# Hash attention and a PReLU feed-forward block: q loaded in blocks and transposed on VectorE, three small jobs moved to GpSimd

## The chip, the cores and the metric

The kernel runs on one NeuronCore of one Trainium2 chip. The metric is the device time of one execution in microseconds (us); a kernel is given by the median of its runs. A profile is one further execution with the hardware profiler on. Engines are called PE (TensorE), DVE (VectorE), ACT (ScalarE), POOL (GpSimd) and SP (SyncE, which here only issues DMAs).

## The reference

```python
# q, k, v: (4, 8, 768, 64) float32; proj: (64, 6)
q_bits = (np.einsum('bhsd,dk->bhsk', q, proj) > 0)
k_bits = (np.einsum('bhsd,dk->bhsk', k, proj) > 0)
# six bits make a bucket number for each query and each key
mask   = q_bucket[:, :, :, None] == k_bucket[:, :, None, :]
scores = np.where(mask, scale * (q @ k^T), -1e9)
attn   = softmax(scores);  x = attn @ v          # heads side by side: (3072, 512)
h      = x @ w_in                                # w_in (512, 2048)
g      = np.maximum(h, 0) + alpha * np.minimum(h, 0)
out    = g @ w_out                               # w_out (2048, 512)
```

A query attends only to keys in the same hash bucket. Six bits of q and of k are signs of a projection.

## The kernel before

There are 4 × 8 heads, handled as 16 **pairs** of heads of 64 columns each, so that a pair fills 128 partitions. The attention stage is one loop over the pairs `pi`; after it come 60 products of the feed-forward block (the first of them begins in the last pair), which the change does not touch.

**One pair on PE.** `scores(pi)` (L755) makes 12 cells, for 6 key tiles `kc` and 2 query groups `g` of 384. Each cell adds a matmul of hash bits (`kb`, `qb`, bf16) to one of `kT` and `qT`; differing bits push the score far down, so that the exponential is nearly zero. ACT takes each cell out of PSUM with one exponential into `pts[kc]` (L766). Then PE does `hash_bits(pi + 1)` (L710, 16 matmuls, tile `hs`), `turn(pi + 2, "q")` (L681, six transposes of 128x128 into PSUM, tile `tp_q`, which ACT copies out with a factor 2^-20 into `qT`), `attend(pi)` (L788, tile `av`, the product with v) and `totals(pi)` (L801, tile `sm`, the row sums from `accd`).

**q and k.** `load` brings both into `nat` two to three pairs ahead. q goes with the sequence in the partitions in two DMAs of 192 KB and is transposed by PE. k has `BY_BLOCKS = 'k'`: `load_blocks` brings it in four DMAs of 96 KB whose runs are 32 numbers long, ordered so that one DVE instruction that transposes 32x32 blocks (`turn_blocks`, L697) gives `kT`. At the end of a pair ACT squares `qn` and `kn` for a bound on their size (`magnitude`), which frees their buffers.

**One pair on DVE, in this order.** Of `divide(pi - 1)`: transposes of the sums `st`, reciprocals and small copies; `weight_clamp` and `weight_parts` for weight tile `i`; `add_first` (`accp` = key tiles 0 + 1); the rest of `divide`, a transpose `dn` and the scaled output `x`; `weight_sum` of `i` (two instructions, L637 and L640) and `weight_clamp` of `i + 1`; `add_third` (L781, `accp` += tile 2); `add_last` (`accd` = tiles 3 + 4, then += 5); `weight_parts` and `weight_sum` of `i + 1`; `add_total` (`accd` += `accp`, read by `totals`); up to two sums of w_in from `weight_sums(2)` (L658, each 128x512); `turn_blocks` of k for `pi + 2`. Four w_in groups exist, with four sums each: they fall due two at a time in pairs 3, 4, 6, 7, 9, 10, 12 and 13. In pairs 3 and 6 the group is completed by that pair's first `weight_sum`, in pairs 9 and 12 by its second; the other four pairs take the two sums that are left of a group completed in the pair before.

**Hash bits.** ACT writes signs for half the bits in place and the rest beside it (L731). Six small DMAs then move bits to the partitions where they belong: four into `qb` (L736) and two inside `kb` (L738). The first score cell of the next pair reads `qb` of group 0, the second cell `qb` of group 1; the two `kb` transfers are for key tiles 3 to 5, from the seventh cell on.

**Order.** `do(...)` pins an instruction behind whatever its engine was given last. A DMA start that is not inside `do` is free: the build's scheduler may issue it earlier, when it takes its inputs to be ready. Each engine then works through its queue in order. All transfers of the attention stage except two at the very beginning are issued by SP; POOL issues DMAs only in the feed-forward stage (`load_out` and `sum_out`, eight each).

Of the kernel before, what the change touches and what calls it, by code (L numbers as in the profile page):

```python
# [12 lines left out]
AF = mybir.ActivationFunctionType  # L13
ALU = mybir.AluOpType
# [393 lines left out]
def fast_path(  # L408
# [12 lines left out]
    nc = tc.nc  # L421
    P = 128
    B, H, S, D = q.shape
# [13 lines left out]
    DOWN = 2.0 ** -20  # L437
# [5 lines left out]
    do = tc.keep_in_program_order  # L443
    PE, DVE, ACT, POOL = nc.tensor, nc.vector, nc.scalar, nc.gpsimd
# [35 lines left out]
    nat, tr, bits = {}, {}, {}  # L480
    accp, accd, av, vsum, sums = {}, {}, {}, {}, {}

    def load(pi, name):
        b, hp = pairs[pi]
        src = {"q": q, "k": k, "v": v}[name]
        if name == "v":
            t = pool.tile([P, 2, NC * D], F32, name=f"vn{pi}", tag="vn")
            nc.sync.dma_start(t, src[b, 2 * hp : 2 * hp + 2].rearrange("h (p c) d -> p h (c d)", c=NC))
            nat[name, pi] = t
        elif pi > 1 and name in BY_BLOCKS:  # L490
            load_blocks(pi, name)
# [8 lines left out]
        for s in range(2):  # L500
            queue.dma_start(nat[name, pi][:, cs, s], src[b, 2 * hp + s].rearrange("(p c) d -> p c d", c=NC)[:, cs])

    BY_BLOCKS = 'k'

    def load_blocks(pi, name):
        b, hp = pairs[pi]
        src = {"q": q, "k": k}[name]
        nat[name, pi] = t = pool.tile([P, NC * 4, 32], F32, name=f"{name}n{pi}", tag=f"{name}n", bufs=3)
        for s in range(2):
            for h in range(2):  # L510
                a = D * s + 32 * h
                nc.sync.dma_start(
                    t[a : a + 32].rearrange("i (c u) d -> i c u d", u=4),
                    src[b, 2 * hp + s, :, 32 * h : 32 * h + 32].rearrange("(u i c) d -> i c u d", u=4, c=NC),
                )
# [39 lines left out]
    raw, wx, wr = {}, {}, {}  # L555
# [22 lines left out]
    def load_weight(i):  # L578
        if i < NW:
            i = order[i]  # L580
            raw[i] = pool.tile([P, 512], moe_w_in.dtype, name=f"raw{i}", tag="raw", bufs=3)
            nc.sync.dma_start(raw[i], piece(i))
# [19 lines left out]
    def weight_clamp(i):  # L602
        if i < NW:
            i = order[i]
            x = wx[i]
            do(DVE.tensor_scalar(x, x, HI_MIN, None, op0=ALU.max, op1=ALU.max, accum_out=wmax[:, i : i + 1]))

    def weight_parts(i):
        i = order[i]
        x = wx[i].bitcast(U32)  # L610
        turned = i < HW and i % 4 == 3
        do(DVE.tensor_scalar(
            x, x, 3, 0x40000000 if turned else 0xC0000000, op0=ALU.logical_shift_left, op1=ALU.bitwise_xor,
        ))
# [29 lines left out]
    def weight_group(i):  # L644

        i = order[i]
        if i >= HW:
            n, m = divmod(i - HW, 2)
            if m == 1:
                nc.sync.dma_start(w_out_r[:, :, n].rearrange("m p d -> p m d"), wst[HW + n])  # L650
            return
        n, m = divmod(i, 4)
        if m < 3:
            return
        w = wst[n]

        def one(to, a, op, c):
            do(DVE.tensor_tensor(w[:, to], w[:, a], w[:, c], op=op))  # L658

        def store():  # L660
            c, kk = divmod(n, 2)
            for ii in range(4):
                nc.sync.dma_start(w_in_s[4 * c + ii][:, :, kk], w[:, :, ii])


        for x in ((3, 5, 2), (5, 0, 5), (4, 3, 0), (6, 1, 4)):
            sums_due.append((one, (x[0], x[1], ALU.subtract, x[2])))
        sums_due.append((store, ()))
# [9 lines left out]
    def two_banks(name):  # L678
        return psum.tile([P, 2, 512], F32, name=name, tag="sc", bufs=3)
# [28 lines left out]
    def hash_bits(pi, halves=BOTH, engine=None):  # L708

        if halves.start == 0:
            bits["q", pi] = qbs[pi % 2]
            kb = pool.tile([P, 3 * CW], BF16, name=f"kb{pi}", tag="kb", bufs=1)
            bits["k", pi] = kb[:, :S]
            bits["raw", pi] = kb.rearrange("p (a w) -> p a w", w=CW)
        ps = {"k": two_banks(f"hs{pi}")}
        ps["q"] = psum_av.tile([P, 2, 512], F32, name=f"hsq{pi}", tag="av") if engine is DVE else ps["k"]
        for half in range(halves.start, halves.stop):
            for name in "qk" if engine is DVE else "kq":  # L720
                for s in range(2):
                    r, c = D * s, D * (s ^ half) + 32 * "kq".index(name)

                    for t, c in [("k", c)] + ([("q", c ^ D)] if engine is DVE and name == "q" else []):
                        do(PE.matmul(
                            ps[t][c : c + 32, half if t == "k" or engine is not DVE else 0, :CW], wh[r : r + D],
                            tr[name, pi][r : r + D, half * CW : (half + 1) * CW], start=True, stop=True,
                        ))
        if engine is None:
            raw = bits["raw", pi]  # L730
            do(ACT.activation(raw[:, 0:3:2], ps["k"][:, :, :CW], AF.Sign, bias=hb))  # L731
            for half in range(2):
                for s in range(2):
                    c = D * (s ^ half)
                    cols = slice(half * CW, (half + 1) * CW)
                    nc.sync.dma_start(bits["q", pi][D * s : D * s + 32, cols], raw[c + 32 : c + 64, 2 * half])  # L736
                    if half:
                        nc.sync.dma_start(bits["k", pi][D * s : D * s + D, cols], raw[c : c + D, 2])  # L738
            return
        for half in range(halves.start, halves.stop):  # L740
            cols = slice(half * CW, (half + 1) * CW)
            for s in range(2):
                c = D * (s ^ half ^ (engine is DVE)) + 32
                do(ACT.activation(
                    bits["q", pi][D * s : D * s + 32, cols], ps["q"][c : c + 32, 0 if engine is DVE else half, :CW], AF.Sign, bias=hb[c : c + 32],
                ))

            for to, c, n in [(0, 0, P)] if half == 0 else [(0, D, D), (D, 0, D)]:
                dst, src = bits["k", pi][to : to + n, cols], ps["k"][c : c + n, half, :CW]
                do(DVE.tensor_scalar(  # L750
                    dst, src, hb_k[c : c + n, 0:1], hb_k[c : c + n, 1:2], op0=ALU.is_gt, op1=ALU.subtract,
                ))
# [16 lines left out]
    def p(kc):  # L769
        return pts[kc].rearrange("p g s w -> p (g s) w")[:, :, :CW]  # L770

    def add_first(pi):
        accp[pi] = pool.tile([P, 2 * NCH, CW], F32, name=f"accp{pi}", tag="accp", bufs=1)
        do(DVE.tensor_tensor(accp[pi], p(0), p(1), op=ALU.add))  # L774
# [4 lines left out]
        do(DVE.tensor_tensor(accd[pi], accd[pi], p(5), op=ALU.add))  # L779

    def add_third(pi):  # L781
        do(DVE.tensor_tensor(accp[pi], accp[pi], p(2), op=ALU.add))  # L782

    def add_total(pi):
        do(DVE.tensor_tensor(accd[pi], accd[pi], accp[pi], op=ALU.add))  # L785
# [375 lines left out]
    for pi in range(NPAIR):  # L1161
        i = 2 * pi

        def weight_begin():
            weight_clamp(i)
            weight_parts(i)
            add_first(pi)

        scores(pi, [c for c in CELLS if pi or c not in ahead])
        if pi:  # L1170
            divide(pi - 1, weight_begin)
        else:
            add_first(pi)
        weight_sum(i)
        weight_group(i)
        load_weight(i + 3)
        if pi == 0:
            weight_abs(1, DVE)
        weight_clamp(i + 1)
        add_third(pi)  # L1180
        add_last(pi)
        weight_parts(i + 1)
        weight_sum(i + 1)
        weight_group(i + 1)
        load_weight(i + 4)
        add_total(pi)
        weight_sums(2)
        if pi + 1 < NPAIR:
            hash_bits(pi + 1)
        if pi + 2 < NPAIR:  # L1190
            for name in "qk":
                (turn_blocks if name in BY_BLOCKS else turn)(pi + 2, name)
        attend(pi)
        if pi + 1 == NPAIR:
            now = ff1(0, 0)
            now.step(1)
        totals(pi)
        if pi + 1 == NPAIR:
            now.step(5)
            divide(pi)  # L1200
        else:
            weight_abs(i + 2)
        if pi + 2 < NPAIR:
            load(pi + 2, "v")
        if pi in (9, 11, 15):
            load_w((9, 11, 15).index(pi))
        if pi in (9, 10, 12):
            load_x(0, *{9: (0,), 10: (2, 3), 12: (1,)}[pi])
        if 11 <= pi < 14 or pi == 15:
            sum_x(0, min(pi - 11, 3), DVE)  # L1210
        if pi == 1:
            setup_alpha()
        for name in "qk":
            magnitude(pi, name)
            if pi + 3 < NPAIR:
                load(pi + 3, name)
        if pi + 1 < NPAIR:
            weight_abs(i + 3)
# [97 lines left out]
```

## Time and profile before

| | us |
|---|---|
| median of 3 runs | 892.92 (892.18 to 896.64) |
| the profiled execution | 890.84 |
| its span, first to last instruction | 888.9 |
| DVE busy, 1280 instructions | 758.2 |
| ACT busy, 654 instructions | 369.1 |
| POOL busy, 30 instructions | 14.4 |
| attention stage, until the first product `f_0a` | 333.6 |
| one DVE transpose of q or k (`kT<-kn`), mean | 0.97 |
| one sum of w_in on DVE (`wsi`), mean | 0.69 |

Busy time is a share of the span by engine; it does not say which engine holds the others up, which is read from the waits and from the order in time. The starts of `add_first` (L774), once per pair, mark the period of the attention loop. In the order of the pairs they are 15.78, 34.94, 55.11, 75.06, 96.19, 116.15, 136.10, 157.40, 177.65, 197.32, 217.27, 237.22, 258.64, 279.35, 300.60 and 320.18 us: 19.95 us in an undisturbed pair, up to 21.4 in others.

### The profile page before, as it was taken

The numbers are of one execution on the slowest core, as the hardware profiler recorded it, in microseconds if no ns is written. First come the engines' busy times: TensorE is split into PE (matmuls) and PEld (weight loads), VectorE is DVE, ScalarE is ACT, GpSimd is POOL, SyncE is SP. The second block draws the span as 40 slices with busy tenths as digits, with TensorE's granted clock in tenths as the row PEclk, the third lists the DMA queues.
The fourth block names the chain that finished last, engine by engine and source line by source line (L and its number), as shares of the span: only waits on it lengthen the run. The fifth ranks groups of instructions, "written<-read, shape, count | busy, mean of one in ns | idle before, by whom it ended". The sixth has DMA issues, their size and how long they took to land.

```text
span 888.9 us, 15214 instructions
## 1 busy us (share of the span) xinstructions
PE 874.4 (98%) x5802; PEld 589.5 (66%) x5802; DVE 758.2 (85%) x1280; ACT 369.1 (42%) x654; POOL 14.4 (2%) x30
## 2 busy tenths in 40 slices
PE   9999999999999999999999999999999999999996
PEld 5444544544444445558996558997557997557996
DVE  5899999899989987899898768898668988668895
ACT  7877777777777743221112222112222112222111
POOL 1000000000000001210000000000000000000000
PEclk9999999999999999999999999999999999999999
DMA  8655686687795616677334434434435343520242
GB/s 219 169 133 137 169 229 158 154 218 210 210 266 153 201 48 222 213 281 289 106 122 118 141 118 157 146 107 125 149 115 163 110 146 87 172 98 1 95 155 63
DMA packets 148130, 137.23 MB, mean 154 GB/s; under 512 B 100928, under 2 KB 132176, under 8 KB 144464
## 3 DMA queue, kind: packets, MB, share of 16 engines
q1 hardware_dynamic: 143328, 126.59, 47.0%
q0 software_dynamic: 2304, 8.39, 2.5%
q10 hardware_dynamic: 2416, 1.18, 0.5%
q8 instruction: 48, 0.79, 0.4%
q14 instruction: 34, 0.28, 0.1%
HBM read 104.87 MB, written 28.31 MB: 150 GB/s over the span
## 4 chain that ended last, share of the span: by engine, by line
PE 83%; DVE 8%; DMA 4%; issue 2%; SPq 1%; ACT 1%; DVEq 0%; ACTq 0%
PE sc L763 12%; PE av L796 10%; PE f_0a L896 2%; PE z_4a L896 2%; PE z_3a L896 2%; PE z_7a L896 2%; PE z_5a L896 2%; PE z_6a L896 2%; PE f_4a L896 2%; PE f_3a L896 2%; PE f_1a L896 2%; PE f_2a L896 2%; PE z_2a L896 2%; PE f_5a L896 2%; PE z_1a L896 2%
## 5 line engine op out<-in xcount | busy, mean ns | idle before, releaser
L766 ACT ACTIVATE pt<-sc 128x768 f32<-128x768 f32 x192 | 154.6, 812 | 47.7 <-PE sc L763 46.9
L763 PE MATMUL sc<-qT,kT 64*128 64x384 f32 x768 | 155.7, 483 | 0.0
L796 PE MATMUL av<-pt,vn 128*32 128x385 f32 (+1 forms) x1536 | 127.4, 486 | 0.0
L763 PEld LDWEIGHTS sc<-qT,kT 64*128 64x128 f32 x768 | 70.0, 187 | 41.5 <-issue 41.1
L796 PEld LDWEIGHTS av<-pt,vn 128*32 128x32 f32 x1536 | 48.9, 109 | 70.9 <-issue 70.1
L763 PE MATMUL sc<-qb,kb 64*128 64x384 bf16 x384 | 66.1, 323 | 4.8 <-DMA qb<-kb 4.1
L949 DVE TENSOR_TENSOR g<-g,g 128x384 f32<-128x384 f32 x128 | 68.4, 555 | 2.2
L1013 DVE TENSOR_TENSOR gs<-g,gs 128x768 f32<-128x768 f32 x56 | 53.3, 953 | 1.0
L1005 DVE TENSOR_TENSOR ws<-wl 128x512 f32<-128x512 f32 x56 | 38.5, 687 | 18.3 <-DMA wl<-w_out_s 17.1
L1013 DVE TENSOR_TENSOR gs<-g 128x768 f32<-128x768 f32 x56 | 53.3, 952 | 0.0
L945 DVE SCALAR_TENSOR_TENSOR g<-h,alpha 128x384 f32<-128x384 f32 x32 | 19.7, 616 | 25.1 <-ACT h L938 25.1
L774 DVE TENSOR_TENSOR accp<-pt,pt 128x1536 f32<-128x1536 f32 x16 | 28.1, 1759 | 13.2 <-ACT pt L766 13.2
L763 PEld LDWEIGHTS <-kb 64*128 64x128 bf16 x384 | 21.0, 94 | 27.7 <-issue 4.4
L596 ACT ACTIVATE wr<-raw 128x512 int32<-128x512 uint32 x32 | 22.8, 711 | 26.6 <-issue 25.8
L779 DVE TENSOR_TENSOR accd<-accd,pt 128x1536 f32<-128x1536 f32 x16 | 28.1, 1759 | 1.7
L782 DVE TENSOR_TENSOR accp<-accp,pt 128x1536 f32<-128x1536 f32 x16 | 28.1, 1753 | 0.0
L785 DVE TENSOR_TENSOR accd<-accd,accp 128x1536 f32<-128x1536 f32 x16 | 28.0, 1752 | 0.0
L778 DVE TENSOR_TENSOR accd<-pt,pt 128x1536 f32<-128x1536 f32 x16 | 28.0, 1751 | 0.0
L896 PE MATMUL f_0a<-x,wi 128*128 128x384 f32 x64 | 23.5, 489 | 0.0
L896 PE MATMUL f_1a<-x,wi 128*128 128x384 f32 x64 | 23.3, 486 | 0.0
L896 PE MATMUL f_4a<-x,wi 128*128 128x384 f32 x64 | 23.3, 486 | 0.0
L896 PE MATMUL f_2a<-x,wi 128*128 128x384 f32 x64 | 23.3, 486 | 0.0
(348 smaller groups left out, 1698.1 us busy)
## 6 DMA issues: line engine op xcount, KB each, us to landing
wi<-w_in_s SPq DMA_DIRECT2D x32, 896.0 KB, 4.7
wl<-w_out_s SPq DMA_DIRECT2D x16, 1024.0 KB, 4.8
wl<-w_out_r SPq DMA_DIRECT2D x12, 1024.0 KB, 4.9
raw<-in_moe_w_out_dram SPq DMA_DIRECT2D x16, 512.0 KB, 4.3
raw<-in_moe_w_in_dram SPq DMA_DIRECT2D x16, 512.0 KB, 4.0
w_in_s<-wsi SPq DMA_DIRECT2D x16, 448.0 KB, 5.4
vn<-in_v_dram SPq DMA_DIRECT2D x16, 384.0 KB, 4.5
x_s<-x SPq DMA_DIRECT2D x16, 384.0 KB, 2.6
```

The costliest lines, as they stand in the source:

```text
L763: do(PE.matmul(sc[:, s, :CW], what["k", pi][r, ks], what["q", pi][r, qs], start=first, stop=not first,))
L766: do(ACT.activation(pts[kc][:, g, :, :CW], sc[:, :, :CW], AF.Exp, scale=SCALE / DOWN))
L774: do(DVE.tensor_tensor(accp[pi], p(0), p(1), op=ALU.add))
L778: do(DVE.tensor_tensor(accd[pi], p(3), p(4), op=ALU.add))
L779: do(DVE.tensor_tensor(accd[pi], accd[pi], p(5), op=ALU.add))
L782: do(DVE.tensor_tensor(accp[pi], accp[pi], p(2), op=ALU.add))
L785: do(DVE.tensor_tensor(accd[pi], accd[pi], accp[pi], op=ALU.add))
L796: do(PE.matmul(av[pi][D * s + t : D * s + t + 32, g, :w], nat["v", pi][:, s, kc * D + t : kc * D + t + 32], pts[kc][:, g, s, :w], start=(k ...
L896: do(PE.matmul(self.ps[bank], self.left(left, k), self.right(right, k), start=start and k == 0, stop=k == self.nk - 1, skip_group_check=no ...
L949: do(DVE.tensor_tensor(new_g(b, to)[:, i], g_m[b, x][:, i], g_m[b, y][:, i], op=ALU.subtract))
L1005: do(DVE.tensor_tensor(t, w2[b, n, x], w2[b, n, y], op=op))
L1013: do(DVE.tensor_tensor(t, g2[b, n, x], g2[b, n, y], op=ALU.subtract))
```

## The change

q joins k in `BY_BLOCKS`. For pairs 2 to 15 q is then loaded by four DMAs instead of two, PE's six transposes per pair and ACT's copy out of PSUM go, and one DVE transpose comes in. The factor 2^-20, which ACT's copy applied, is applied by an ACT instruction on `qT` in place, after the hash matmuls have read it. The six hash-bit DMAs of a pair are issued by POOL instead of SP. Two kinds of addition move from DVE to POOL: the sums of w_in and `add_third`.

```diff
-    BY_BLOCKS = 'k'
+    BY_BLOCKS = 'qk'
...
         def one(to, a, op, c):
-            do(DVE.tensor_tensor(w[:, to], w[:, a], w[:, c], op=op))
+            do(POOL.tensor_tensor(w[:, to], w[:, a], w[:, c], op=op))
...
                     cols = slice(half * CW, (half + 1) * CW)
-                    nc.sync.dma_start(bits["q", pi][D * s : D * s + 32, cols], raw[c + 32 : c + 64, 2 * half])
+                    nc.gpsimd.dma_start(bits["q", pi][D * s : D * s + 32, cols], raw[c + 32 : c + 64, 2 * half])
                     if half:
-                        nc.sync.dma_start(bits["k", pi][D * s : D * s + D, cols], raw[c : c + D, 2])
+                        nc.gpsimd.dma_start(bits["k", pi][D * s : D * s + D, cols], raw[c : c + D, 2])
...
     def add_third(pi):
-        do(DVE.tensor_tensor(accp[pi], accp[pi], p(2), op=ALU.add))
+        do(POOL.tensor_tensor(accp[pi], accp[pi], p(2), op=ALU.add))
...
         if pi + 1 < NPAIR:
             hash_bits(pi + 1)
+            if pi:
+                do(ACT.activation(tr["q", pi + 1], tr["q", pi + 1], AF.Copy, scale=DOWN))
         if pi + 2 < NPAIR:
             for name in "qk":
                 (turn_blocks if name in BY_BLOCKS else turn)(pi + 2, name)
```

## The prediction

> **What bounds the kernel now.** I read the page first: busy shares and the chain.
>
> ```profile
> PE 874.4 (98%) x5802; PEld 589.5 (66%) x5802; DVE 758.2 (85%) x1280; ACT 369.1 (42%) x654; POOL 14.4 (2%) x30
> ...
> PE 83%; DVE 8%; DMA 4%; issue 2%; SPq 1%; ACT 1%; DVEq 0%; ACTq 0%
> ```
>
> PE holds the chain for 83%, so work taken from PE can shorten the span. The 8% of DVE and 4% of DMA warn that something else ends close behind. The change touches only the attention loop, so next comes the timeline of one undisturbed pair (pair 2), PE and then DVE.
>
> ```profile
> 61.35 0.88 PE L690 MATMUL tp_q<-ident,qn 128*128 128x128 f32 x6
> 62.16 7.96 PE L796 MATMUL av<-pt,vn 128*32 128x385 f32 x96
> 69.94 0.84 PE L810 MATMUL sm<-accd,ones 128*32 128x192 f32 x16
> ```
>
> ```profile
> 55.11 1.76 DVE L774 TENSOR_TENSOR accp<-pt,pt 128x1536 f32<-128x1536 f32 x1 [0.88 <-ACT pt L766]
> ...
> 58.73 0.68 DVE L637 SCALAR_TENSOR_TENSOR wx<-raw,wx 128x512 uint32<-128x512 uint32 x1
> ...
> 60.66 1.75 DVE L782 TENSOR_TENSOR accp<-accp,pt 128x1536 f32<-128x1536 f32 x1
> ...
> 67.65 1.75 DVE L785 TENSOR_TENSOR accd<-accd,accp 128x1536 f32<-128x1536 f32 x1
> 69.32 0.97 DVE L699 STREAM_TRANSPOSE kT<-kn 128x768 f32<-128x768 f32 x1
> 70.83 0.65 DVE L826 STREAM_TRANSPOSE st<-sm 128x192 f32<-128x192 f32 x2 [0.55 <-PE sm L810]
> ```
>
> From tp_q's start to av's is 0.81 us: what PE pays per pair for transposing q. DVE ends add_total at 67.65 + 1.75 = 69.40, PE starts the sums that read it at 69.94: DVE is only 0.54 early, less than 0.81. In the whole loop of 19.95 us DVE idles 0.88 + 0.55 = 1.4. Pair 14 has no q to turn, so it shows what PE meets without tp_q:
>
> ```profile
> 306.85 7.96 PE L796 MATMUL av<-pt,vn 128*32 128x385 f32 x96
> 315.03 0.86 PE L810 MATMUL sm<-accd,ones 128*32 128x192 f32 x16 [0.21 <-DVE accd L785]
> ```
>
> It waits 0.21 for accd. DVE's chain, not ACT or a DMA, is next, and the answer depends on whether moving add_third really shortens it. Last, waits and DMA issues:
>
> ```profile
> PE sc L763 <- DMA qb<-kb: 4.1, 4, 1.2
> ```
>
> ```profile
> w_out_r<-wso SPq DMA_DIRECT2D x8, 512.0 KB, 4.7
> wo<-w_out_r POOLq DMA_DIRECT2D x8, 512.0 KB, 6.7
> w_out_s<-wo POOLq DMA_DIRECT2D x8, 512.0 KB, 5.6
> qb<-kb SPq DMA_DIRECT2D x60, 24.0 KB, 3.1
> ```
>
> Hash bits are late four times (4.1 us in all), because SP stands at a weight load or store that waits for DVE. POOL's transfers take 0.9 to 2.4 us longer to land than SP's 4.3 to 4.7 for the same size; POOL's own timeline has four issued in 3.12, so 0.78 each.
>
> **What the Trainium skill says.** (1) "SBUF — State Buffer", section "Who interferes with whom": a DVE instruction with two SBUF inputs contends with a GpSimd instruction that reads SBUF, and the one that comes second is blocked until the first is done; a DVE instruction with one SBUF input outside the two-port modes is not. The trace before has no POOL arithmetic in the loop and can't confirm it. (2) "GPSIMD Engine Reference", section 3.1: an fp32 tensor_tensor of 2048 takes 4497 ns on GpSimd against 2293 on DVE. The DVE half fits (1.75 us for 1536 here); the other isn't shown. (3) "DMA: Bandwidth & Descriptors", "SWDGE vs HWDGE vs iDMA": DMAs from GpSimd have their descriptors made by its cores in software; the slower landing above agrees.
>
> **The change, part by part** (L774 starts F are the clock of a pair, S is the start of its scores, F = S + 4.3.)
>
> *q's transposes off PE:* 14 pairs x 0.81 = 11.3 us less PE. ACT's copy (0.80) becomes a copy in place, like the SBUF-to-SBUF pass L706 (0.85): 14 x 0.05, on an engine that idles 1.8 us in the same stretch: nothing. It ends some 7 us before the next scores; without that cover 0.85 per pair.
>
> *q's DVE transpose:* +0.97, after add_total and before the sums are read (st). It fills the 0.55 idle there; the remaining 0.4 comes out of the 0.88 idle ahead of add_first. So nothing, as long as add_total isn't later.
>
> *q's loads:* four issues of about 0.65 instead of two, minus six hash issues (0.58 each): SP gains 2 us per pair. The data are wanted a pair later (about 20 us, landing 3.4 to 4): nothing. The DMA engines were busy 54 to 97% of each pair; 128-byte runs instead of 256 add packets, not bytes. Below 1 us of DMA time per pair, I take nothing.
>
> *Hash bits on POOL:* the signs are ready at S + 11.7. The fifth transfer is the last for qb: four issues x 0.78 later, plus landing. Low bound 3.1 as from SP; high 3.1 + 2.4 = 5.5; I take 4.0 (3.1 + 0.9, the stores' difference): S + 18.8, wanted in the second cell at S + 19.15 + 0.8 = S + 19.95. They fit by 1.1; the 4.1 us of SP's lateness go. POOL's queue ahead of them holds add_third and, in eight pairs, two sums.
>
> *add_third on POOL:* 1536/2048 x 4.5 = 3.4 us (estimate from the skill's GPSIMD page; low bound 1.75 as on DVE). It starts when add_first is done, F + 1.9, and ends F + 5.3. DVE meanwhile does dn and x (one SBUF input each) and comes to L637 at F + 3.62 (58.73 - 55.11), which reads raw and wx, two SBUF inputs: held for 1.7. What the move removes is 1.67 (60.66 to 62.33). Net +0.03: nothing gained on DVE. If nothing is held, -1.67.
>
> *Descriptors:* POOL's six issues lie at F + 7.5 to F + 12.2, and the tensor_scalar L612 (0.42 us for 512, so in a two-port mode) comes at F + 10.7. Held 0 to 0.78, I take 0.3.
>
> *Sums of w_in on POOL:* 512 wide: 1.1 us each. In pairs 4, 7, 10 and 13 they are ready and follow add_third at once, just where DVE goes through L637, L640 (two inputs) and a clamp (one); in pairs 3 and 6 they follow L640 and meet add_last. Taking turns, DVE loses 2 x 1.1 less the 0.6 of the clamp, 1.6. In pairs 9 and 12 they meet add_total: one of them ahead of it, 1.1. DVE's saving of 1.41 comes after add_total, where it only becomes idle time. Low bound nothing.
>
> **The sum.** add_total ends F + 14.29 (69.40 - 55.11) now, F + 14.29 + 0.03 + 0.3 = F + 14.6 after. From there two transposes (1.94) and the row from st to L612 (3.3) to the next F: 19.85, against 19.95. Six early-sum pairs 21.45, pairs 9 and 12 20.95, pair 1 (alpha) 20.05, pair 0 19.0. From the first F to the last: 19.0 + 20.05 + 5 x 19.85 + 6 x 21.45 + 2 x 20.95 = 308.9. Now: 320.18 - 15.78 = 304.4. So +4.5, and 0.3 for pair 15: +4.8. The profiled execution took 890.84 (span 888.9 and 1.9 around it) and would take 895.6; the median of the runs is 2.1 above it, so 897.7.
>
> **Forecast and rivals.**
> - *DVE is held by POOL (forecast, 0.45):* 898, 890 to 908. For it: the 0.21 wait of pair 14 and DVE's 1.4 us of idle per loop. Within it 0.27 slower, 0.17 within, 0.01 faster.
> - *POOL and DVE run side by side (0.30, the other side):* one mechanism, no blocking at L637. add_total ends at F + 12.6, before PE needs it (F + 14.0); PE bounds again: -11.3 - 4.1 gives 877.5, 873 to 884. For it: no trace here shows blocking. The point of decision is the hold: below about 0.7 us per pair DVE keeps ahead of PE. 0.28 faster, 0.02 within.
> - *Hash bits become the bound (0.25):* issues 1.2 apart or queued behind sums, landing 5.5: S + 11.7 + 4.8 + 5.5 = S + 22.0, 2.05 late, 15 times: 31. Less 15.4 gives 908.5, 903 to 930. Against: 0.78 per issue of a transfer twenty times larger. For it: POOL's queue is in order and a DVE that wins every turn starves the sums and with them the bits behind. 0.24 slower, 0.01 within.
>
> Faster 0.29, within 0.20, slower 0.51. 0.5% is 4.5 us, about what a measurement of this kernel can tell from no change. The range 876 to 915 leaves out the fast end of the second case and half of the third, under 0.2; the forecast's own is 890 to 908.
>
> **What would show it.** Right: no tp_q, period near 19.9 in plain pairs and over 21 with sums, L637 with idle time ahead of it or stretched by 1 to 2 us while POOL works, PE waiting for accd at L810. Second case: L637 at F + 3.6 and periods of 19.2. Third: scores waiting on `qb<-kb` in most pairs. What would make it wrong: a POOL add nearer 2 us, or 5.

## The result and the profile after

The changed kernel takes 891.27 us (median of 20 runs, 890.25 to 895.57), the kernel before 892.22 (20 runs beside them): a ratio of 0.9991, 95% interval 0.9978 to 1.0003. That is no change that can be measured. The profiled execution took 891.28; its span is 889.4 us, 0.5 more than before.

The page of the changed kernel: the chain by engine, then three groups with count, busy us, mean ns, and the idle time before them.

```profile
PE 71%; DVE 12%; ACT 6%; issue 4%; DMA 3%; POOL 3%; SPq 0%; DVEq 0%; ACTq 0%; POOLq 0%
...
L782 POOL TENSOR_TENSOR accp<-accp,pt 128x1536 f32<-128x1536 f32 x16 | 51.1, 3194 | 164.1 <-DVE accp L774 164.1
...
L637 DVE SCALAR_TENSOR_TENSOR wx<-raw,wx 128x512 uint32<-128x512 uint32 x32 | 42.3, 1322 | 0.5
...
L658 POOL TENSOR_TENSOR wsi<-wsi 128x512 f32<-128x512 f32 x16 | 29.3, 1834 | 8.5 <-DVE wsi L640 8.0
```

PE's share of the chain fell from 83% to 71%; DVE, ACT and POOL took most of it over. L637 did not change in the source, but its mean went from 688 to 1322 ns. That is the trace of an instruction that is held, which means that it waits while it is counted as running: every other L637 (the one of tile `i`) runs beside `add_third`. Pair 2 in time, DVE and then POOL:

```profile
54.41 1.76 DVE L774 TENSOR_TENSOR accp<-pt,pt 128x1536 f32<-128x1536 f32 x1 [0.45 <-ACT pt L766]
...
58.03 2.04 DVE L637 SCALAR_TENSOR_TENSOR wx<-raw,wx 128x512 uint32<-128x512 uint32 x1
...
66.65 1.75 DVE L785 TENSOR_TENSOR accd<-accd,accp 128x1536 f32<-128x1536 f32 x1
```

```profile
56.35 3.17 POOL L782 TENSOR_TENSOR accp<-accp,pt 128x1536 f32<-128x1536 f32 x1 [10.42 <-DVE accp L774]
62.07 1.50 POOL L736 DMA_DIRECT2D qb<-kb  x3 [2.55 <-ACT kb L731]
```

POOL's add runs from 56.35 to 59.52. L637 begins at 58.03 and ends at 60.07, 0.55 after POOL: nearly all of its own 0.68 comes when the add is over. It is held 1.36 us. `add_total` starts 12.24 after L774, against 12.54 before: of the 1.67 that left DVE, 1.37 came back as waiting.

In pair 3 the two sums of w_in meet `add_last` (DVE, then POOL):

```profile
80.61 2.46 DVE L778 TENSOR_TENSOR accd<-pt,pt 128x1536 f32<-128x1536 f32 x1
83.17 2.65 DVE L779 TENSOR_TENSOR accd<-accd,pt 128x1536 f32<-128x1536 f32 x1
```

```profile
80.16 4.04 POOL L658 TENSOR_TENSOR wsi<-wsi 128x512 f32<-128x512 f32 x2 [1.36 <-DVE wsi L640]
```

Both additions of 1.75 are stretched, by 0.71 and 0.89, and POOL's two sums take 4.04 where 2.62 is enough (the gated kernel below). The two engines take turns here, and `add_total` comes 1.6 later than in pair 2. Pair 9 goes another way (POOL, then PE):

```profile
205.02 0.52 POOL L738 DMA_DIRECT2D kb<-kb  x1
208.17 2.72 POOL L658 TENSOR_TENSOR wsi<-wsi 128x512 f32<-128x512 f32 x1 [2.63 <-DVE wsi L640]
210.85 0.52 POOL L736 DMA_DIRECT2D qb<-kb  x1
```

```profile
211.51 0.32 PE L763 MATMUL sc<-qb,kb 64*128 64x384 bf16 x1
214.50 0.32 PE L763 MATMUL sc<-qb,kb 64*128 64x384 bf16 x1 [2.67 <-DMA qb<-kb]
```

Here the build put a sum between the fourth and the fifth hash-bit transfer. The sum waits for L640, then for `add_total` (208.00 to 209.75), and the last `qb` transfer stands behind it: the second score cell is 2.67 late.

Pair 12 has the same order on POOL, and its second score cell is 1.70 late. But its length comes from somewhere else: there DVE has a sum of x behind the transposes (L868, in pairs 11 to 13), which takes 0.95 alone and is held by the second sum of w_in:

```profile
274.30 2.05 DVE L868 TENSOR_TENSOR x<-x,x 128x768 f32<-128x768 f32 x1
```

DVE has no idle time in this pair before it comes to the next `add_first`, where it idles 0.36, as in a plain pair. So DVE's work, with this hold in it, is as long as the pair (21.28). The late bits can have cost 0.24 at most: the third score cell needs DVE to be done with `st` (276.91, behind L868), and starts at 277.15.

### The profile page after: what moved, and what is told of

It reads as the page before. It is cut to its first block, busy times and chain, and to the rows that moved or that the text cites. A ratio compares the mean times of both kernels' runs of the same rounds, so it can differ in the third digit from the quotient of the medians.

```text
span 889.4 us, 15185 instructions
## 1 busy us (share of the span) xinstructions
PE 864.7 (97%) x5718; PEld 577.0 (65%) x5718; DVE 766.4 (86%) x1262; ACT 370.1 (42%) x654; POOL 140.7 (16%) x152
## 4 chain that ended last, share of the span: by engine, by line
PE 71%; DVE 12%; ACT 6%; issue 4%; DMA 3%; POOL 3%; SPq 0%; DVEq 0%; ACTq 0%; POOLq 0%
PE sc L763 7%; ACT pt L766 5%; PE av L796 4%; PE f_0a L896 2%; PE z_4a L896 2%; PE z_7a L896 2%; PE z_3a L896 2%; PE z_6a L896 2%; PE z_5a L896 2%; PE f_4a L896 2%; PE f_3a L896 2%; PE f_2a L896 2%; PE f_1a L896 2%; PE z_2a L896 2%; PE f_5a L896 2%
## 5 line engine op out<-in xcount | busy, mean ns | idle before, releaser
L782 POOL TENSOR_TENSOR accp<-accp,pt 128x1536 f32<-128x1536 f32 x16 | 51.1, 3194 | 164.1 <-DVE accp L774 164.1
L637 DVE SCALAR_TENSOR_TENSOR wx<-raw,wx 128x512 uint32<-128x512 uint32 x32 | 42.3, 1322 | 0.5
L774 DVE TENSOR_TENSOR accp<-pt,pt 128x1536 f32<-128x1536 f32 x16 | 28.1, 1758 | 8.5 <-ACT pt L766 8.2
L736 POOL DMA_DIRECT2D qb<-kb x60 | 30.2, 506 | 23.0 <-ACT kb L731 20.5
L779 DVE TENSOR_TENSOR accd<-accd,pt 128x1536 f32<-128x1536 f32 x16 | 29.9, 1870 | 2.0 <-ACT wr L596 0.5
L778 DVE TENSOR_TENSOR accd<-pt,pt 128x1536 f32<-128x1536 f32 x16 | 31.4, 1963 | 0.0
L658 POOL TENSOR_TENSOR wsi<-wsi 128x512 f32<-128x512 f32 x16 | 29.3, 1834 | 8.5 <-DVE wsi L640 8.0
```

The source lines that it names most:

```text
L637: do(DVE.scalar_tensor_tensor(x.bitcast(U32), hi, 0x80000000, x.bitcast(U32), op0=ALU.bitwise_and, op1=ALU.bitwise_xor,))
L736: nc.gpsimd.dma_start(bits["q", pi][D * s : D * s + 32, cols], raw[c + 32 : c + 64, 2 * half])
L778: do(DVE.tensor_tensor(accd[pi], p(3), p(4), op=ALU.add))
L782: do(POOL.tensor_tensor(accp[pi], accp[pi], p(2), op=ALU.add))
```

## The experiments

Periods are the distances between the starts of `add_first` in each profile, so each comes from one execution; "loop" is the sum of the 15. A plain pair is pair 2; pair 4 is one with sums. The kernels ran in three groups (e1 to e4, e5 to e8, e9 and e10), each beside runs of the kernel before; ratios are against those.

| kernel | us | ratio (95%) | loop | plain pair | pair 4 |
|---|---|---|---|---|---|
| before | 892.22; beside the three groups 893.94, 893.66, 893.28 | | 304.4 | 19.95 | 19.96 |
| changed | 891.27 | 0.9991 (0.9978 to 1.0003) | 304.9 | 19.28 | 20.72 |
| e1_sums_dve | 886.91 | 0.9930 (0.9906 to 0.9953) | 300.7 | 19.28 | 20.39 |
| e2_q_and_bits | 889.90 | 0.9957 (0.9940 to 0.9973) | 303.9 | 19.59 | 20.69 |
| e3_q_alone | 906.88 | 1.0150 (1.0120 to 1.0179) | 317.8 | 19.65 | 20.69 |
| e4_bits_alone | 887.31 | 0.9933 (0.9909 to 0.9957) | 299.8 | 19.95 | 19.95 |
| e5_sums_gated | 879.29 | 0.9846 (0.9825 to 0.9868) | 293.3 | 19.28 | 19.24 |
| e6_sums_behind_bits | 900.14 | 1.0082 (1.0062 to 1.0102) | 311.1 | 19.29 | 21.64 |
| e7_write_only (sums incomplete) | 874.20, one run | | 288.2 | 19.14 | 19.14 |
| e8_one_input (sums incomplete) | 884.21, one run | | 297.8 | 19.14 | 20.18 |
| e9_gated_clamp | 877.15 | 0.9824 (0.9811 to 0.9837) | 290.3 | 19.14 | 19.15 |
| e10_sum_x_pool | 874.93 | 0.9795 (0.9781 to 0.9808) | 288.9 | 19.14 | 19.15 |

**Taking the change apart.** The diffs of e1 to e3 are against the changed kernel, that of e4 against the kernel before.

```diff
 # e1_sums_dve
-            do(POOL.tensor_tensor(w[:, to], w[:, a], w[:, c], op=op))
+            do(DVE.tensor_tensor(w[:, to], w[:, a], w[:, c], op=op))
 # e2_q_and_bits: that, and
-        do(POOL.tensor_tensor(accp[pi], accp[pi], p(2), op=ALU.add))
+        do(DVE.tensor_tensor(accp[pi], accp[pi], p(2), op=ALU.add))
 # e3_q_alone: both, and the hash bits' two DMA starts
-                    nc.gpsimd.dma_start(...)
+                    nc.sync.dma_start(...)
 # e4_bits_alone: the kernel before, with both DMA starts
-                    nc.sync.dma_start(...)
+                    nc.gpsimd.dma_start(...)
```

> The changed kernel with the sums of w_in back on DVE. Port theory (GpSimd's two-input adds hold DVE's two-input instructions): plain pairs stay at 19.3 us; the eight pairs with sums carry 1.33 of sums on DVE and no hold but add_third's, 20.2 instead of 20.7 to 22.3; pairs 9 and 12 lose their late hash bits. 299 instead of 305 for the loop: 885. Rival, GpSimd's queue (the hash bits behind add_third and the sums cost the time): all pairs near 19.3, 878. Rival, DVE's length alone decides (nothing is held, the sums cost nothing on GpSimd): slower than the changed kernel, 896.

> The changed kernel with both additions back on DVE, so q in blocks and the hash bits on GpSimd remain. Port theory: add_third costs DVE 1.67 instead of a hold of 1.37, so plain pairs take 19.6 and pairs with sums 20.6: 302 for the loop, 889 to 890. L637 is back at 0.69. Rival, GpSimd's queue: without arithmetic in it the bits are on time everywhere, all pairs 19.3, 878. Rival, DVE's length: 1.7 to 3 us per pair more on DVE than in the changed kernel, 900 or more.

> Only q in blocks, everything else as before. Port theory and DVE's length: PE loses 0.81 per pair, but add_total on DVE ends 14.3 after add_first and DVE has one transpose more; plain pairs 19.6, pairs with sums 20.6, and the hash bits from SP are late as before (about 4 in all): 893 to 894, no gain. If PE alone bounded the loop: 881.

> The kernel before with only the hash bits moved to GpSimd. If SP's place in line made them late, the waits of the scores for qb and kb (4.1 us) go and the five long pairs (21.1 to 21.4) fall to 20: 887. If GpSimd's issue or landing is slower than SP's, they stay or grow: 893 or more.

The first and second came out within 2 us of the number of the port theory (GpSimd's additions hold DVE's two-input instructions), and the fourth within 1 us of what it should take if SP's place in line made the bits late. Both rivals fell as the main cause: with no arithmetic in POOL's queue (e2) the pairs with sums are not at 19.3, and with more work on DVE (e1, e2) the kernel is not slower than the changed one. Read as steps of the loop: bits to POOL, 304.4 to 299.8 (-4.6); q in blocks on top, 303.9 (+4.1); `add_third` to POOL, 300.7 (-3.2); the sums to POOL, 304.9 (+4.2). The four cancel. Each step holds for this order alone, and with the other parts as they stand in it: with the bits still on SP, q in blocks costs 13.4 of loop instead of 4.1 (e3). The medians of the runs give -6.6, +2.6 and -3.0 for the first three steps: the same signs, and within 2 us of the loops.

The step with q surprises most. PE lost its 0.81 per pair, and the plain pairs of e2 gained 0.36; but in a pair with sums DVE had little idle (0.27 in e4 at the end of pair 4), and the transpose of 0.97 made pair 4 0.74 longer. In e2 DVE has no idle time at all there. The transpose stands ahead of `st`, and PE shows it as a wait of the third score cell, because `sm`, which `st` reads, and the score cells take turns in the same three PSUM buffers:

```profile
PE sc L763 <- DVE st L826: 9.7, 9, 1.8
```

In e4 this wait is 1.2 in two. It is 0.94 in each of pairs 3, 4, 6, 7, 9 and 10 of e2, and 1.81 in pairs 12 and 13, where a sum of x comes on top. A transpose placed behind `st` was not tried. With the sums taken off DVE and gated (e5, below) these pairs take 19.24 to 19.29: what costs is the transpose together with sums on DVE.

e3 missed its number by 13 us. Its waits on PE name the hash bits, 16.6 us in nine waits; the worst is in pair 11 (SP, then PE):

```profile
248.67 0.59 SPq L663 DMA_DIRECT2D w_in_s<-wsi  x1
254.67 0.38 SPq L650 DMA_DIRECT2D w_out_r<-wso  x1
255.47 0.33 SPq L582 DMA_DIRECT2D raw<-in_moe_w_out_dram  x1
255.85 2.73 SPq L663 DMA_DIRECT2D w_in_s<-wsi  x3
258.68 3.71 SPq L736 DMA_DIRECT2D qb<-kb  x3
```

```profile
264.49 0.58 PE L763 MATMUL sc<-qb,kb 64*128 64x384 bf16 x2 [7.17 <-DMA qb<-kb]
```

The signs were ready at 249.4 (ACT's L731), but SP stood at the store of `wso`, which waits for DVE until 254.64; it issued that store and four more transfers, and the first of the bits only at 258.68. After the wait the granted clock was only 0.50 (264 to 268 us; 1.00 from 270), and pair 11 took 29.48, 9.25 more than in e2. Why the build ordered SP's queue so unluckily in this pair was not followed up; that the bits' place in SP's queue is the danger is what e4 shows from the other side: on POOL, no wait of the scores for bits is left, and of the long pairs of before (21.1 to 21.4) pairs 3, 6 and 11 are at 19.95 and pair 13 at 20.70.

**Where the sums stand.** Two kernels leave them on POOL and move them in its queue. `gate` is a small tile that nothing reads (its declaration is left out here).

```diff
 # e6_sums_behind_bits; e5_sums_gated has the gate too
-        weight_sums(2)
         if pi + 1 < NPAIR:
             hash_bits(pi + 1)
             if pi:
                 do(ACT.activation(tr["q", pi + 1], tr["q", pi + 1], AF.Copy, scale=DOWN))
+        if sums_due and sums_due[0][0].__name__ == "one":     # e5 alone
+            do(POOL.tensor_copy(gate, accd[pi][:, 0, :1]))    # e5 alone
+        weight_sums(2)
```

> The changed kernel with the sums of w_in still on GpSimd, but queued behind the pair's hash bits and behind a one-column copy of accd, which waits for add_total. They then run while DVE does transposes and small one-input instructions. Port theory: no hold but add_third's, all pairs near 19.3, loop 290 instead of 305: 876 to 878. GpSimd's queue as the cause: the same, since the bits are ahead of the sums. DVE's length: no change against the changed kernel, 891.

> As the gated kernel without the gate: sums on GpSimd behind the pair's hash bits, with nothing to make them wait for add_total. They run beside the second half of add_last, weight_sum and add_total. Port theory: DVE is held 1.2 to 1.5 there, pairs with sums 20.6, but pairs 9 and 12 are rid of late bits: 887 to 888. GpSimd's queue as the cause: bits are never behind sums, 878, the same as with the gate.

They differ by one small copy on POOL, and by 21 us. The queue rival wanted them equal; it is out, as is the length of DVE's work, which is the same in both. The gated kernel in pair 3 (POOL, then DVE; its line numbers are two higher):

```profile
87.69 0.18 POOL L1194 COPY gate<-accd 128x1 f32<-128x1 f32 x1 [3.08 <-DVE accd L787]
87.83 2.62 POOL L660 TENSOR_TENSOR wsi<-wsi 128x512 f32<-128x512 f32 x2
```

```profile
87.54 0.97 DVE L701 STREAM_TRANSPOSE qT<-qn 128x768 f32<-128x768 f32 x1
88.44 0.93 DVE L701 STREAM_TRANSPOSE kT<-kn 128x768 f32<-128x768 f32 x1
89.30 0.60 DVE L828 STREAM_TRANSPOSE st<-sm 128x192 f32<-128x192 f32 x2
89.93 0.54 DVE L829 TENSOR_SCALAR rc<-st 128x12 f32<-128x12 f32 x1
```

Two sums take 2.62 instead of 4.04, DVE's transposes run beside them at their own length, and the only thing held is a small one, L829 (0.54 instead of 0.17). Pairs 2 to 10 take 19.24 to 19.29, as expected. Pairs 11 to 13 do not, because of the sum of x on DVE: 19.89, and in pairs 12 and 13, where it meets the gated sums and takes up to 2.02 instead of 0.95, 21.04 and 20.95. Pair 3 without the gate, in e6 (DVE, then POOL):

```profile
84.01 1.93 DVE L612 TENSOR_SCALAR wx<-wx 128x512 uint32<-128x512 uint32 x1
85.97 1.65 DVE L637 SCALAR_TENSOR_TENSOR wx<-raw,wx 128x512 uint32<-128x512 uint32 x1
```

```profile
84.35 2.72 POOL L658 TENSOR_TENSOR wsi<-wsi 128x512 f32<-128x512 f32 x2
```

L612 (0.42 alone) is held by 1.5 and L637 by 0.96, which ends 0.55 behind the second sum.

The port theory's own expectation, 887 to 888, missed by 12, for two reasons. First, it counted two-input instructions alone, and L612 has one. The Trainium skill's page "SBUF — State Buffer", section "Who interferes with whom", says that a DVE instruction in a two-port mode contends with GpSimd too, and names `tensor_scalar` among those that can be; the 1.93 of L612 agrees. `add_total` came 2.4 later than in a plain pair, and PE waited 15.1 us for it in seven pairs.

Second, in pairs 7, 10 and 13 the granted clock fell to 0.50 after that wait (from 176 to 178 us, in pair 7), and four score matmuls took 1.49 instead of 0.81. These pairs took 23.4; pairs 3, 4 and 6, with waits of 2.3 to 2.4 and a clock of 1.00 after them, took 21.6 to 21.8. So some 5 of the 21 us (an estimate, three times 23.4 - 21.7) go with the lower clock. Why it fell in three pairs alone was not followed up.

**What on POOL holds DVE.** Two kernels replace `add_third` by work on POOL that only writes, or that reads one input; the sums of w_in are on DVE. The row sums then leave out key tiles, so these kernels are for the trace alone; each has one run.

```diff
-        do(POOL.tensor_tensor(accp[pi], accp[pi], p(2), op=ALU.add))
+        for i in range(3):
+            do(POOL.memset(accp[pi], 0.0))             # e7_write_only
...
+        for i in range(2):
+            do(POOL.tensor_copy(accp[pi], p(2)))       # e8_one_input
```

> add_third is replaced by three GpSimd memsets of accp at the same place, sums on DVE: the row sums leave out key tiles 0 to 2. Three memsets of 1536 take about 4 us from add_first's end, so they cover L637. If only reads of GpSimd hold DVE's two-input instructions, L637 stays at 0.69 us. If any GpSimd access to SBUF holds them, L637 is stretched by 0.7 or more.

> add_third is replaced by two GpSimd copies of key tile 2 into accp at the same place, sums on DVE: the row sums leave out key tiles 0 and 1. If one read stream on GpSimd is enough to hold DVE, L637 is stretched until the copy that runs beside it ends; if it takes two input streams, L637 stays at 0.69 us.

Write only (POOL, DVE), then one input (POOL, DVE):

```profile
55.59 4.25 POOL L783 MEMSET accp<- 128x1536 f32 x3 [10.41 <-DVE accp L774]
```

```profile
57.32 0.68 DVE L637 SCALAR_TENSOR_TENSOR wx<-raw,wx 128x512 uint32<-128x512 uint32 x1
```

```profile
56.03 3.00 POOL L783 COPY accp<-pt 128x1536 f32<-128x1536 f32 x2 [10.46 <-DVE accp L774]
```

```profile
57.73 1.84 DVE L637 SCALAR_TENSOR_TENSOR wx<-raw,wx 128x512 uint32<-128x512 uint32 x1
```

Writes of POOL leave L637 at 0.68, though they lie over all of it. One stream of reads is enough to hold it, until POOL's work ends at 59.03: 57.73 + 1.84 is 0.54 later, as with the add. e7 also shows the floor: without a hold, and with the sums on DVE, 11 of the 15 periods are 19.14 to 19.15, which is PE's own length (busy for 19.14 of 19.14 in pair 2), and the loop takes 288.2.

**A better version.** e9 moves `weight_clamp(i + 1)` ahead of `weight_sum(i)` in the gated kernel; e10 also gives POOL the sums of x of pairs 11 to 13.

```diff
+        if pi:
+            weight_clamp(i + 1)
         weight_sum(i)
...
         if pi == 0:
             weight_abs(1, DVE)
-        weight_clamp(i + 1)
+            weight_clamp(i + 1)
         add_third(pi)
...
 # e10_sum_x_pool
-        if sums_due and sums_due[0][0].__name__ == "one":
+        if sums_due and sums_due[0][0].__name__ == "one" or 11 <= pi < 14:
             do(POOL.tensor_copy(gate, accd[pi][:, 0, :1]))
...
-            sum_x(0, min(pi - 11, 3), DVE)
+            sum_x(0, min(pi - 11, 3), POOL if pi < 14 else DVE)
```

> The gated kernel with the one-input weight_clamp of i + 1 moved ahead of weight_sum of i, so that DVE has 0.6 us more of work that add_third cannot hold. Port theory: the hold on L637 falls from 1.37 to 0.7, add_total comes 11.6 after add_first, and PE bounds the plain pairs at 19.15: 2 us less than the gated kernel, 877. If DVE is held for add_third's whole length whatever stands there: no change, 879.

> As e9, and three sums of x (128x768, in pairs 11 to 13) go to GpSimd behind the gate too; on DVE they were held for 1.0 by the gated sums of w_in. Port theory: pairs 11 to 13 fall from 19.9, 21.0 and 21.0 to about 19.3: 4 us less than e9, 873 to 874. If the longer stay of GpSimd in that gap holds L612 or add_first of the next pair, 1 to 2 us of it come back.

In e9 L637 (there L639) starts after the clamp and is shorter by just what the clamp took of the hold:

```profile
58.66 1.45 DVE L639 SCALAR_TENSOR_TENSOR wx<-raw,wx 128x512 uint32<-128x512 uint32 x1
```

The plain period is PE's 19.14. e9 and e5 ran in different groups and their ratios' intervals overlap; the loop is 3.0 shorter. In e10 pairs 11 and 13 fell to 19.15 and 19.79 and pair 12 only to 20.20 (e9: 19.30, 20.36 and 20.46): 1.5 us of loop instead of 4. The expectation had named POOL's longer stay in that gap as a cost that would fall on L612 or `add_first`. The trace shows it, on another instruction. In pair 12 (DVE, then POOL):

```profile
262.75 1.39 DVE L834 COPY rr<-rr 32x12 f32<-32x12 f32 x1
```

```profile
262.29 1.82 POOL L870 TENSOR_TENSOR x<-x,x 128x768 f32<-128x768 f32 x1
```

L834, a copy with one input that takes 0.16 alone, ends with POOL's sum of x (264.14 and 264.11); in pair 13 it takes 1.38. Pair 11 has no sums of w_in ahead of the sum of x, and there nothing is held. At 0.9795 of before, e10 is still the fastest kernel that computes the whole result.

## Why the prediction was wrong, point by point

The forecast was 898 us, slower; measured 891.27, which is within the range but not the slowdown that was forecast. Its case, DVE held by POOL, is the one that happened. The step that failed is the size of what DVE loses in a plain pair: 1.7 of hold and 0.3 of descriptors against the 1.67 that `add_third` leaves. The hold measured 1.36 and the descriptors nothing, so `add_total` ends earlier than before and not later. Of the 6.4 us between 897.7 and 891.27, 4.0 are loop (308.9 against 304.9) and 2.1 the distance from the profiled execution to the median, which was added from three runs of the kernel before and was nothing in the changed one.

- *DVE is next after PE, and POOL's reads hold its two-input instructions:* right, shown by L637 and by e7, e8, e5 and e6. The Trainium skill's page "SBUF — State Buffer", section "Who interferes with whom", says that reads are what contends with two inputs, and e7 and e8 agree.
- *The hold in a plain pair, 1.7:* mis-sized, 1.36. POOL's add took 3.19 (estimate 3.4) and starts at F + 1.94 as expected. With the next point this is the failed step: "F + 14.29 + 0.03 + 0.3 = F + 14.6" measured F + 12.24 + 1.75 = F + 14.0.
- *Descriptors hold L612, 0.3:* wrong, nothing. L612 keeps 0.42 beside POOL's transfers. In pair 2 it is one POOL transfer that takes 0.72 instead of 0.52.
- These two terms put the plain pairs at 19.85 instead of 19.28, and were carried into every other pair: 14 times 0.57 is 8.0 too long. It is luck that the loop was only 4.0 too long: the late bits of pair 9 and the sums of x, neither of them in the forecast, made up for most of the rest.
- *Six pairs with early sums, 1.6 more:* right in size (pair 3: 20.88 - 19.28 = 1.60; pair 4: 1.44), but for pair 13, which has a sum of x as well (21.37).
- *Pairs 9 and 12, 1.1 by holding add_total:* the wrong mechanism. `add_total` won and held the sum. In pair 9 a hash-bit transfer waited behind it: 22.25 instead of 20.95. The rival had named bits queued behind sums, but for all pairs. In pair 12 (21.28) it is the held sum of x that counts.
- *Sums of x:* not in the forecast's sum, though the kernel before has them too. They make pair 11 19.91 instead of 19.28.
- *Hash bits on POOL fit by 1.1, and 4.1 us of lateness go:* right in the plain pairs and in e4 (4.6 of loop), though by other numbers: 0.50 per issue instead of 0.78, landing 3.0 instead of 4.0. The term of 0.9 taken from the stores of 512 KB did not carry over to 24 KB.
- *q's DVE transpose "fills the idle", so nothing:* right where the sums are off DVE, as the forecast had them: plain pairs, and in e5 the pairs with sums too. It rests on that: with the sums on DVE the transpose costs 0.74 in a pair with sums (e2 against e4).
- *The other side (877.5 if nothing is held)* did not happen in the changed kernel. e5 reaches 879.3 with most of the hold of the sums taken away; e9, where the hold on L637 is 0.77, has plain pairs at PE's 19.14, close to the 0.7 that the prediction named as the point of decision.

## What to carry to other kernels

Work given to GpSimd is not free for VectorE: what counts is which of VectorE's instructions stand beside it, so place it, by a true dependency if need be, over VectorE's transposes, and look for unchanged instructions that became longer. One input alone is no protection: L612, L829 and the copy L834 were held too. A change of several parts with a net of nothing is worth taking apart: here parts worth -4.6, +4.1, -3.2 and +4.2 us, in the order taken, cancelled, and moving one of them behind the bits and a gate in its queue gave 12 us. Small transfers that the next stage needs soon should not share an in-order queue with anything that waits for a slow producer, be it stores on SP or sums on GpSimd.

## What the runs showed of the hardware that was not expected

Without the gate, two GpSimd adds in a row ran through almost undelayed (2.72 us) and VectorE waited behind each; beside VectorE's additions of 1.75 both sides waited (4.04). In the first case L612 is on record from 84.01, 0.34 before the first sum; it did not get done ahead of it. What decides who goes first was not tried. A transfer of 24 KB issued by GpSimd costs it 0.50 us and landed no later than one from SP (medians 3.0 and 3.1, in e4 2.1), while for 512 KB GpSimd's took 5.6 to 6.7 to land and SP's 4.0 to 4.7; those come at other times of the kernel, so that the issuer is the cause is not shown.

The granted clock fell to 0.50 after waits of PE of 2.4 us in e6 (three pairs of six) and of 7.2 in e3, and stayed there for about 3 us each time in e6, and from about 260 to 269 us in e3. It was 1.00 after the wait of 2.67 in the changed kernel. A late input can thus cost more than its lateness.
